# ScalarE copies of the FFN half tiles in batch 0, and accumulator banks lent to batch 1's first transposes

## The chip, the cores and the metric

One Trainium2 chip, of which the kernel uses a single core. The metric is the device time of one execution in microseconds (us); below two or three runs of the same kernel their median is given. A core has five engines that run side by side, each in its own program order: TensorE (PE, matrix products, its weight loads shown as PEld), VectorE (DVE), ScalarE (ACT), GpSimd (POOL) and SyncE (SP, which here issues nearly all DMAs).

## The reference

Inputs: `q`, `k`, `v` of shape (8 batches, 8 heads, 576 positions, 64), `p` of shape (8, 8, 32, 64), and two weight matrices `w_in` (512 x 2048) and `w_out` (2048 x 512) that arrive as 64-bit floats. All results are 32-bit.

```python
p_packed = sm_attn(p, k, v)              # 32 packed rows attend to 576 keys
out = sm_attn(q, p_packed, p_packed)     # 576 queries attend to the 32 packed rows
x = out.transpose(0, 2, 1, 3).reshape(B * S, H * D)        # 4608 x 512
h = x @ w_in
g = maximum(h, 0) + log1p(exp(-abs(h)))  # softplus
return g @ w_out
```

## The kernel before, in words

**The work.** The eight batches are taken one after the other. For a batch, `attention(b)` makes the softmaxed attention weights of the second attention (`aT`, split into a high and a low part `at_h`, `at_l` by `weights`), and `make_m` folds the packed rows into `w_in` (tiles `mh`, `ml`), so that the FFN's first product `h` is `m` times `at`. The FFN then runs over 16 tiles `f` of 128 hidden columns. Every large product is made of three products of rounded parts (high x high, high x low, low x high).

**A unit.** The main loop goes over units `u`, each a pair (batch, f); unit 0 is batch 0's tile 0 and unit 16 is batch 1's tile 0. In each unit these things are issued, in this order:

1. `gemm1` (line 581): 12 matmuls into two PSUM banks `ph`, one for each half of 288 positions. The pool `ps_h` has exactly two banks, so the next unit's `gemm1` writes the same two.
2. `softplus`, a chain of steps. Line 603: ScalarE takes `Abs` of each half out of PSUM into `e`. Lines 605 and 606: `Exp` and `Ln` on `e`, for batch 0 over both halves at once. Line 608: VectorE takes `max(h, 0) + e`, and reads `h` for it out of `ph` once more, so that both banks are held until line 608 has run. Later steps copy 64 columns aside on GpSimd (line 612) and split `e` into `gh` and `gl` on VectorE (lines 595, 596).
3. `gemm2_tile` (line 619) for the unit two before (`LAG = 2`): four accumulator tiles `acc`, 12 matmuls of 512 columns. The four banks of `ps_acc` hold them for a whole batch.
4. Between these four tiles, steps of the next batch's attention (`ahead`), and in batch 0 steps of `convert`.
5. After the unit, `make_m` for the unit two ahead, whenever a new slice of `m` begins: in batch 0 every second unit, 256 columns at a time (`psm`, line 544; read by ScalarE at line 559 and by VectorE at line 560).

**The PSUM banks.** Eight in all: four for `acc`, two for `ph`, and two (`ps_m`, tag "m") that everything else shares through `bank(...)`: the attention's transposes and scores, and `psm`. Before the first unit the list `spare` lends the accumulator banks to batch 0's attention; it is emptied (`spare.clear()`) ahead of unit 0.

**Batch 1's attention** runs inside batch 0's units. It begins with `transposed("k", 1, 0, hh)` for four `hh`: three transposes on TensorE (line 263) into one bank, and a ScalarE copy out of it (line 269, tile `T_k`). Two of them fall in unit 0, two in unit 1; the first scores that use them (line 276) come in unit 2, where the tiles `acc` of batch 0 are allocated too.

**The conversion.** `convert` turns the 64-bit weights into the 32-bit ones, 32 pieces in a fixed order (two of `w_in`, then two of `w_out`, and so on). A piece is a DMA into a buffer, two ScalarE activations (200, 204), two VectorE operations (206, 211), one GpSimd add (219), and for `w_out` another ScalarE (238) and VectorE (244) operation. It begins before unit 0 and ends in batch 0's last units.

**The order.** TensorE's instructions run in the order in which the program writes them. On the other engines a scheduler orders the instructions when the kernel is built, by priority (the order of the program) and by when it expects operands to be ready; on the chip each engine then runs its list in order. SyncE issues the loads in that way too.

Of the kernel before, what the change touches and what calls it, by code (L numbers as in the profile page):

```python
# [9 lines left out]
F32 = mybir.dt.float32  # L10
F32R = mybir.dt.float32r
AF = mybir.ActivationFunctionType
ALU = mybir.AluOpType
AX = mybir.AxisListType
I32 = mybir.dt.int32
# [11 lines left out]
def pack_attention_then_softplus_ffn(  # L27
# [10 lines left out]
    nc = tc.nc  # L38
    B, H, S, D = q.shape
    J = p.shape[2]  # L40
    DM, DFF = w_in.shape
    P = 128
# [3 lines left out]
    C = S // 2  # L46
# [9 lines left out]
    scale = 1.0 / math.sqrt(D)  # L56
# [4 lines left out]
    work = ctx.enter_context(tc.tile_pool(name="work", bufs=2))  # L61
    small = ctx.enter_context(tc.tile_pool(name="small", bufs=2))
    ps_acc = ctx.enter_context(tc.tile_pool(name="ps_acc", bufs=NT, space=bass.MemoryType.PSUM))
# [13 lines left out]
    def rest_at(b, f):  # L77

        return f + NF if f < LAG and b // 2 % 2 else f
# [3 lines left out]
    pT = const.tile([P, H, PW], F32, name="pT")  # L83

    spare = []

    def bank(nm):
        if spare:
            spare.append(spare.pop(0))
            pool, tag = spare[-1]  # L90
            return pool.tile([P, 512], F32, tag=tag, name=nm)
        return ps_m.tile([P, 512], F32, tag="m", name=nm)
# [24 lines left out]
    def load(nm, b, g):  # L117
        if b >= B:
            return
        src = {"q": q, "k": k, "v": v}[nm][b, g * HG:(g + 1) * HG]  # L120
        if b < FIRST:
            if (nm, b) == ("q", 0):
                o = DFF - (g + 1) * SI * D
                t = w_in_sb[:NP, :, o:o + SI * D].rearrange("x h (s d) -> x h s d", d=D)
            else:
                t = ld.tile([NP, HG, SI, D], F32, tag="ld", name=f"{nm}_{b}_{g}")
            nc.sync.dma_start(
                t.rearrange("x h s d -> x h (s d)"),
                src.rearrange("h (x s) d -> x h (s d)", s=SI),
            )  # L130
        elif nm == "v":
            t = ld.tile([NP, HG, SI, D], F32, tag="ld", name=f"{nm}_{b}_{g}")
            nc.sync.dma_start(
                t.rearrange("x h (m c) d -> x (h m) (c d)", c=2),
                src.rearrange("h (m x c) d -> x (h m) (c d)", x=NP, c=2),
            )
        else:
            t = ld.tile([P, HG, C], F32, tag="ld", name=f"{nm}_{b}_{g}")
            by_quad = src.rearrange("h (n x c) (e d) -> c e x (h n) d", x=Q, c=2, d=Q)
            for i in range(P // Q):  # L140
                nc.sync.dma_start(
                    t[i * Q:(i + 1) * Q].rearrange("x h (n d) -> x (h n) d", d=Q),
                    by_quad[i // 2, i % 2],
                )
        loaded[nm, b, g] = t
# [112 lines left out]
    def transposed(nm, b, g, hh):  # L258

        src = loaded[nm, b, g]  # L260
        ps = bank(f"psT_{nm}_{b}_{g}_{hh}")
        for i in range(HS):
            nc.tensor.transpose(
                ps[:, i * NP:(i + 1) * NP],
                src[:, hh, 2 * i:2 * i + 2, :].rearrange("x s d -> x (s d)"),
                ident[:NP, :NP],
            )
        dst = work.tile([P, C], F32, tag="T", name=f"T_{nm}_{b}_{g}_{hh}", bufs=4)
        nc.scalar.copy(dst, ps[:, :C])  # L269
        return dst  # L270
# [245 lines left out]
    def attention(b):  # L516
        return attention_first(b) if b < FIRST else attention_next(b)
# [18 lines left out]
    def make_m(b, c, res):  # L536


        n = m_cols(b)
        pss = [bank(f"psm_{b}_{c}_{g}") for g in range(G)]  # L540
        for g, ps in enumerate(pss):
            for hh in range(HG):
                o = D * g
                nc.tensor.matmul(  # L544
                    ps[hh * J:(hh + 1) * J, :n],
                    res["pt"][g][o:o + D, hh * J:(hh + 1) * J],
                    w_in_sb[o:o + D, hh, c * n:(c + 1) * n],
                    start=True, stop=True,
                )
        pool, th, tl = (cv, "t", "r") if b and c % 2 == 0 else (work, "mh", "ml")  # L550
        halves = []
        for g, ps in enumerate(pss):
            o = g * n % MC
            if o == 0:
                mh = pool.tile([P, MC], F32R, tag=th, name=f"mh_{b}_{c}_{g}", bufs=2)
                ml = pool.tile([P, MC], F32R, tag=tl, name=f"ml_{b}_{c}_{g}", bufs=2)
                halves.append((mh, ml))
            cols = slice(o, o + n)
            nc.scalar.copy(mh[:, cols], ps[:, :n])  # L559
            nc.vector.tensor_tensor(  # L560
                ml[:, cols], ps[:, :n], mh[:, cols].bitcast(F32), op=ALU.subtract
            )
        res["m"][c] = halves
# [24 lines left out]
    def halves(nm):  # L588
        return [
            work.tile([P, NT * P], F32R, tag=t, name=f"{t}_{nm}", bufs=LAG + 1)  # L590
            for t in ("gh", "gl")
        ]

    def split(hi, lo, x):
        nc.vector.tensor_copy(hi, x)  # L595
        nc.vector.tensor_tensor(lo, x, hi.bitcast(F32), op=ALU.subtract)  # L596

    def softplus(b, f, hv, done):
        e = work.tile([P, S], F32, tag="e", name=f"e_{b}_{f}")
        es = [e[:, c * C:(c + 1) * C] for c in range(2)]  # L600
        spans = [e] if b == 0 else es
        for c in range(2):
            nc.scalar.activation(es[c], hv[c], AF.Abs)  # L603
            for x in spans[c:c + 1] if b else spans[:c]:
                nc.scalar.activation(x, x, AF.Exp, scale=-1.0)  # L605
                nc.scalar.activation(x, x, AF.Ln, bias=1.0)  # L606
        for c in range(2):
            nc.vector.scalar_tensor_tensor(es[c], hv[c], 0.0, es[c], op0=ALU.max, op1=ALU.add)  # L608
        yield
        yield  # L610
        r = (b % 2) * REST
        nc.gpsimd.tensor_copy(rest[:, rest_at(b, f), r:r + REST], e[:, NT * P:])  # L612
        yield
        done[b, f] = halves(f"{b}_{f}")
        split(*done[b, f], e[:, :NT * P])
# [58 lines left out]
        order.append(("o", f))  # L674
    PACE = 0.56
    FRONT = 1000
    PACE_FIRST = 0.62
    CONV = 1.6
    CONV_EARLY = 1.6
# [18 lines left out]
    for st in range(NF * NT):  # L698
        with tc.high_priority(offset=FRONT):
            if next(steps, steps) is steps:  # L700
# [5 lines left out]
    for nm in ("k", "v"):  # L706
        for g in range(G):
            load(nm, 1, g)
    with tc.high_priority(offset=FRONT):
        make_m(0, 0, res[0])  # L710
# [4 lines left out]
    gs, acc = {}, None  # L715
    units = [(b, f) for b in range(B) for f in range(NF)]
    ahead, chain, due = iter(()), iter(()), 0.0
    for u in range(len(units) + LAG):
        if u < len(units):
            b, f = units[u]  # L720
            if f == 0:
                if (b + 1) % BG == 0 and b + 1 < B:
                    pack_transposed((b + 1) // BG, pt)
                ahead = attention(b + 1) if b + 1 < B else iter(())
                due = 0.0
            chain = softplus(b, f, gemm1(b, f, res[b]), gs)
            next(chain)
            if f == NF - 1:
                if (b + 2) % BG == 0 and b + 2 < B:
                    pt = load_pack((b + 2) // BG, (nc.sync,))  # L730
                for _ in ahead:
                    pass
                if b + 1 < B:
                    weights(b + 1)
        if u >= LAG:
            b2, f2 = units[u - LAG]
            gh, gl = gs.pop((b2, f2))
            if f2 == 0:
                acc = [ps_acc.tile([P, DM], F32, tag="acc", name=f"acc_{b2}_{t}") for t in range(NT)]
        last = u >= LAG and f2 == NF - 1 and b2 % 2 == 1  # L740
        if last:
            both = rests(b2)
            next(both)
        for t in range(NT):
            if u >= LAG:
                gemm2_tile(
                    acc[t], gh, gl, f2, slice(t * P, (t + 1) * P), f2 == 0, f2 == NF - 1
                )
                if f2 == NF - 1:
                    store(acc[t], [(0, b2, t * P, P)], f"{b2}_{t}", t)  # L750
            if u < len(units):
                due += PACE if b != FIRST - 1 else PACE_FIRST
                while due >= 1:
                    next(ahead, None)
                    due -= 1
                if b == 0:
                    cdue += CONV
                    while cdue >= 1:
                        next(conv, None)
                        cdue -= 1  # L760
            next(chain, None)
        if last:
            next(both)
        if u + 2 < len(units):


            nb, c = units[u + 2][0], units[u + 2][1] * P
            if c % m_cols(nb) == 0:
                make_m(nb, c // m_cols(nb), res[nb])
# [29 lines left out]
```

## Time and profile before

| | |
|---|---|
| time, median of 3 runs | 772.9 us (772.86 to 773.84) |
| the profiled execution | 772.78 us, its span 771.0 us |
| mean granted TensorE clock | 0.973 of full speed |
| TensorE busy | 733.0 us, 95% of the span |
| VectorE busy | 527.6 us, 68% |
| ScalarE busy | 434.8 us, 56% |
| GpSimd busy | 99.1 us, 13% |
| DMA | 55.97 MB moved, mean 73 GB/s |

The shares are means over the whole span. Batch 0 (its first `gemm1` starts at 39.16 us, batch 1's first at 151.55 us) looks different from the seven batches after it, so the table tells little of the stage that the change touches; that stage has to be read from views with a time window. Times of a view count from the span's start.

### The profile page before, as it was taken

The numbers are of one execution on the slowest core, as the hardware profiler recorded it, in microseconds if no ns is written. First come the engines' busy times: TensorE is split into PE (matmuls) and PEld (weight loads), VectorE is DVE, ScalarE is ACT, GpSimd is POOL, SyncE is SP. The second block draws the span as 40 slices with busy tenths as digits, with TensorE's granted clock in tenths as the row PEclk, the third lists the DMA queues.
The fourth block names the chain that finished last, engine by engine and source line by source line (L and its number), as shares of the span: only waits on it lengthen the run. The fifth ranks groups of instructions, "written<-read, shape, count | busy, mean of one in ns | idle before, by whom it ended". The sixth has DMA issues, their size and how long they took to land.

```text
span 771.0 us, 14168 instructions
## 1 busy us (share of the span) xinstructions
PE 733.0 (95%) x5360; PEld 579.5 (75%) x5360; DVE 527.6 (68%) x1092; ACT 434.8 (56%) x1057; POOL 99.1 (13%) x166
## 2 busy tenths in 40 slices
PE   6657998999999999999999999999999999999997
PEld 3445775887787778878788777878787777888886
DVE  2697879965877569565967559575867558565554
ACT  5668877766454545565555455565555355555540
POOL 1143444200000000000000000000010000000110
PEclk9559999999999999999999999999999999999999
DMA  9978655434403341052302342052402400010002
GB/s 211 237 185 190 185 137 150 95 76 73 93 1 76 56 81 44 1 124 47 79 1 76 55 64 61 1 109 42 91 2 61 70 1 1 1 55 1 1 1 68
DMA packets 149668, 55.97 MB, mean 73 GB/s; under 512 B 116320, under 2 KB 142944, under 8 KB 149600
## 3 DMA queue, kind: packets, MB, share of 16 engines
q1 hardware_dynamic: 149328, 55.00, 31.9%
q8 instruction: 42, 0.69, 0.4%
q14 instruction: 26, 0.21, 0.1%
q10 hardware_dynamic: 272, 0.07, 0.0%
HBM read 45.61 MB, written 9.44 MB: 71 GB/s over the span
## 4 chain that ended last, share of the span: by engine, by line
PE 85%; DVE 6%; ACT 4%; DMA 3%; issue 1%; POOL 1%; SPq 0%; ACTq 0%; DVEq 0%; POOLq 0%
PE acc L619 42%; PE ph L581 26%; PE acc_m L619 6%; PE psm L544 4%; PE ps L276 2%; DMA w_in_sb<-in_q 2%; PE psp L319 2%; PE psa L309 1%; DVE at_l L527 1%; DVE e L608 1%; DVE t L206 1%; ACT e L605 1%; DVE t L211 1%; ACT e L603 1%; DMA k<-in_k 1%
## 5 line engine op out<-in xcount | busy, mean ns | idle before, releaser
L603 ACT ACTIVATE e<-ph 128x288 f32<-128x288 f32 x256 | 103.2, 404 | 190.4 <-PE ph L581 143.4
L619 PE MATMUL acc<-wo_h,gh 128*128 128x512 f32 x512 | 208.0, 406 | 0.0
L608 DVE SCALAR_TENSOR_TENSOR e<-ph,e 128x288 f32<-128x288 f32 x256 | 113.4, 451 | 132.4 <-ACT e L606 131.3
L619 PE MATMUL acc<-wo_l,gh 128*128 128x512 f32 x512 | 201.2, 393 | 0.0
L619 PE MATMUL acc<-wo_h,gl 128*128 128x512 f32 x512 | 201.0, 393 | 0.0
L581 PE MATMUL ph<-at_h,mh 128*128 128x288 f32 x512 | 159.0, 311 | 12.7 <-ACT at_h L526 6.6
L581 PE MATMUL ph<-at_l,mh 128*128 128x288 f32 x512 | 153.6, 300 | 3.7 <-DVE at_l L527 3.7
L581 PE MATMUL ph<-at_h,ml 128*128 128x288 f32 x512 | 152.9, 299 | 0.0
L581 PEld LDWEIGHTS ph<-at_h,mh 128*128 128x128 f32 x512 | 97.9, 191 | 46.7 <-DVE gl L596 9.6
L612 POOL COPY rest<-e 128x64 f32<-128x64 f32 x128 | 53.8, 420 | 577.3 <-DVE e L608 547.7
L619 PEld LDWEIGHTS acc<-wo_h,gh 128*128 128x128 f32 x512 | 96.4, 188 | 27.5 <-issue 10.2
L619 PEld LDWEIGHTS acc<-wo_h,gl 128*128 128x128 f32 x512 | 96.3, 188 | 21.1
L605 ACT ACTIVATE e<-e 128x288 f32<-128x288 f32 (+1 forms) x240 | 109.4, 456 | 4.0
L606 ACT ACTIVATE e<-e 128x288 f32<-128x288 f32 (+1 forms) x240 | 109.4, 456 | 3.2
L619 PEld LDWEIGHTS acc<-wo_l,gh 128*128 128x128 f32 x512 | 96.6, 189 | 13.1
L581 PEld LDWEIGHTS ph<-at_l,mh 128*128 128x128 f32 x512 | 98.1, 192 | 8.1 <-DVE at_l L527 5.3
L581 PEld LDWEIGHTS ph<-at_h,ml 128*128 128x128 f32 x512 | 98.1, 192 | 0.0
L596 DVE TENSOR_TENSOR gl<-e,gh 128x512 fp32r<-128x512 f32 x128 | 87.7, 685 | 5.5
L559 ACT CAST mh<-psm 128x512 fp32r<-128x512 f32 (+1 forms) x72 | 35.9, 539 | 54.5 <-PE psm L544 54.3
L595 DVE CAST gh<-e 128x512 fp32r<-128x512 f32 x128 | 55.5, 434 | 5.5 <-DVE e L608 0.5
L560 DVE TENSOR_TENSOR ml<-psm,mh 128x512 fp32r<-128x512 f32 (+1 forms) x72 | 42.8, 623 | 20.6 <-ACT mh L559 20.0
L544 PE MATMUL psm<-w_in_sb,pt 64*32 64x512 f32 (+1 forms) x576 | 41.3, 567 | 7.6 <-ACT T_k L269 4.8
(79 smaller groups left out, 696.4 us busy)
## 6 DMA issues: line engine op xcount, KB each, us to landing
v<-in_v SPq DMA_DIRECT2D x16, 576.0 KB, 4.9
x_i<-in_moe_w_in SPq DMA_DIRECT2D x28, 256.0 KB, 4.4
k<-in_k SPq DMA_DIRECT2D x48, 144.0 KB, 3.2
q<-in_q SPq DMA_DIRECT2D x48, 144.0 KB, 3.1
x_o<-in_moe_w_out SPq DMA_DIRECT2D x11, 512.0 KB, 3.8
out<-o SPq DMA_DIRECT2D x18, 256.0 KB, 2.5
rest<-in_moe_w_out SPq DMA_DIRECT2D x5, 512.0 KB, 6.1
k<-in_k SPq DMA_DIRECT2D x4, 576.0 KB, 6.7
```

Of the source, the lines that this page charges most:

```text
L544: nc.tensor.matmul(ps[hh * J:(hh + 1) * J, :n], res["pt"][g][o:o + D, hh * J:(hh + 1) * J], w_in_sb[o:o + D, hh, c * n:(c + 1) * n], start ...
L559: nc.scalar.copy(mh[:, cols], ps[:, :n])
L560: nc.vector.tensor_tensor(ml[:, cols], ps[:, :n], mh[:, cols].bitcast(F32), op=ALU.subtract)
L581: nc.tensor.matmul(ph[:, :C], x[:, ms], y[:, g, cs], start=(i == 0), stop=(i == 3 * G - 1),)
L595: nc.vector.tensor_copy(hi, x)
L596: nc.vector.tensor_tensor(lo, x, hi.bitcast(F32), op=ALU.subtract)
L603: nc.scalar.activation(es[c], hv[c], AF.Abs)
L605: nc.scalar.activation(x, x, AF.Exp, scale=-1.0)
L606: nc.scalar.activation(x, x, AF.Ln, bias=1.0)
L608: nc.vector.scalar_tensor_tensor(es[c], hv[c], 0.0, es[c], op0=ALU.max, op1=ALU.add)
L612: nc.gpsimd.tensor_copy(rest[:, rest_at(b, f), r:r + REST], e[:, NT * P:])
L619: nc.tensor.matmul(acc, x[:, cs], y[:, f, :], start=(first and i == 0), stop=(last and i == 2),)
```

## The change

Two edits.

- **`softplus` in batch 0** (`OUT = 16`, so all its tiles). ScalarE copies both halves of `ph` into an SBUF tile `x` of 576 columns. VectorE takes the absolute value of all of `x` in one instruction, by masking the sign bit, into `e`. ScalarE's `Exp` and `Ln` follow as before. VectorE's last step is one instruction of 576 columns over `x` and `e`, in place of two of 288 that read `ph`. The tiles `x` use buffers of the attention that lie idle then: those of `aT` for f below 9, those of `a1` from 9 on. Batches 1 to 7 are as they were.
- **`transposed` in batch 1**, as long as `fresh` is not empty, that is until unit 2 allocates `acc`: its transposes go to the four banks of `ps_acc` in place of the two shared ones. Four such tiles fall in that time, one for each bank.

```diff
+    fresh = [None]
...
     def transposed(nm, b, g, hh):
         src = loaded[nm, b, g]
-        ps = bank(f"psT_{nm}_{b}_{g}_{hh}")
+        if b and fresh:
+            ps = ps_acc.tile([P, 512], F32, tag="acc", name=f"psT_{nm}_{b}_{g}_{hh}")
+        else:
+            ps = bank(f"psT_{nm}_{b}_{g}_{hh}")
...
-    def softplus(b, f, hv, done):
+    def softplus(b, f, phs, done):
+        hv = phs
         e = work.tile([P, S], F32, tag="e", name=f"e_{b}_{f}")
         es = [e[:, c * C:(c + 1) * C] for c in range(2)]
         spans = [e] if b == 0 else es
-        for c in range(2):
+        if b == 0 and f < OUT:
+            x = work.tile(
+                [P, S], F32, tag="aT" if f < 9 else "a1", name=f"x_{b}_{f}", bufs=2
+            )
+            hv = [x[:, c * C:(c + 1) * C] for c in range(2)]
+            for c in range(2):
+                nc.scalar.copy(hv[c], phs[c])
+            nc.vector.tensor_scalar(
+                e.bitcast(I32), x.bitcast(I32), 0x7FFFFFFF, None, op0=ALU.bitwise_and
+            )
+            nc.scalar.activation(e, e, AF.Exp, scale=-1.0)
+            nc.scalar.activation(e, e, AF.Ln, bias=1.0)
+            hv, es, spans = [x], [e], []
+        for c in range(2 if spans else 0):
             nc.scalar.activation(es[c], hv[c], AF.Abs)
             for x in spans[c:c + 1] if b else spans[:c]:
                 nc.scalar.activation(x, x, AF.Exp, scale=-1.0)
                 nc.scalar.activation(x, x, AF.Ln, bias=1.0)
-        for c in range(2):
-            nc.vector.scalar_tensor_tensor(es[c], hv[c], 0.0, es[c], op0=ALU.max, op1=ALU.add)
+        for x, y in zip(es, hv):
+            nc.vector.scalar_tensor_tensor(x, y, 0.0, x, op0=ALU.max, op1=ALU.add)
...
+    OUT = 16
...
             if f2 == 0:
+                fresh.clear()
                 acc = [ps_acc.tile([P, DM], F32, tag="acc", name=f"acc_{b2}_{t}") for t in range(NT)]
```

## The prediction

> **What bounds the kernel now.** I read the page's head first, then busy times by stage, then TensorE's waits in batch 0, then the rows of the engines around each wait.
>
> ```profile
> span 771.0 us, 14168 instructions
> PE 733.0 (95%) x5360; PEld 579.5 (75%) x5360; DVE 527.6 (68%) x1092; ACT 434.8 (56%) x1057; POOL 99.1 (13%) x166
> ```
>
> The sum below is made against this execution: span 771.0, time 772.78, so 1.8 us lie around the span; it is 0.1 below the median of 772.9. By stage (column two is the length, then the busy time of each engine and the granted clock):
>
> ```profile
> core 0: us, PE busy (x) PEld busy (x) DVE busy (x) ACT busy (x) POOL busy (x), PEclk, DMA share, GB/s
> 39.00:66.00 27.00, 16.00 (x86) 11.90 (x87) 22.41 (x34) 17.11 (x35) 12.47 (x10) 0.60 0.81 192
> 66.00:101.00 35.00, 32.71 (x268) 23.99 (x266) 29.18 (x62) 30.99 (x69) 15.98 (x15) 1.00 0.67 176
> 101.00:152.00 51.00, 47.53 (x369) 36.31 (x370) 45.81 (x95) 37.77 (x77) 18.44 (x19) 0.97 0.53 129
> 152.00:760.00 608.00, 606.76 (x4368) 486.07 (x4367) 409.40 (x853) 325.04 (x828) 46.08 (x113) 1.00 0.23 48
> ```
>
> From 152 us on TensorE is busy for 606.76 of 608 us: it is the bound there, and a microsecond by which batch 1's FFN starts earlier or later is a microsecond of the result. All that the change can do is done between 39 and 152 us. There TensorE is idle for 11.0, 2.3 and 3.5 us in the three stages, and the other engines are no longer idle company: VectorE is busy for 97.4 of 113 us, ScalarE for 85.9. TensorE's waits from 39 to 152 us, largest causes:
>
> ```profile
> PE ph L581 <- DVE e L608: 6.0, 4, 3.1
> PE psm L544 <- ACT T_k L269: 4.8, 2, 2.8
> PE psm L544 <- POOL w_in_sb L219: 1.7, 1, 1.7
> ```
>
> The first two rows, 10.8 us, are what the two edits are aimed at: `ph` held until line 608, and `psm` held up by a shared bank that a `T_k` copy has not emptied. Where they sit (start, length, engine, line; in brackets the idle time in front):
>
> ```profile
> 46.33 1.16 PE L263 MATMUL psT_k<-ident,k 96*128 96x96 f32 x6
> 50.28 1.08 PE L544 MATMUL psm<-w_in_sb,pt 64*32 64x256 f32 x8 [2.79 <-ACT T_k L269]
> 53.35 1.08 PE L544 MATMUL psm<-w_in_sb,pt 64*32 64x256 f32 x8 [1.98 <-ACT T_k L269]
> 54.36 0.61 PE L581 MATMUL ph<-at_h,mh 128*128 128x288 f32 x1
> ...
> 57.23 0.66 PE L263 MATMUL psT_k<-ident,k 96*128 96x96 f32 x6
> 60.95 0.61 PE L581 MATMUL ph<-at_h,mh 128*128 128x288 f32 x1 [3.05 <-DVE e L608]
> ...
> 63.93 0.39 PE L619 MATMUL acc<-wo_h,gh 128*128 128x512 f32 x1
> ...
> 75.53 0.40 PE L581 MATMUL ph<-at_h,mh 128*128 128x288 f32 x1 [1.81 <-DVE e L608]
> ...
> 77.23 0.40 PE L619 MATMUL acc<-wo_h,gh 128*128 128x512 f32 x1
> ...
> 134.27 0.67 PE L544 MATMUL psm<-w_in_sb,pt 64*32 64x256 f32 x16 [1.65 <-POOL w_in_sb L219]
> ```
>
> The two waits for `e` not shown make up the rest of the 6.0: 6.0 - 3.05 - 1.81 = 1.1 us.
>
> **Part 1, the lent banks.** What the four first `T_k` copies and the halves' reads looked like on ScalarE, and what VectorE and GpSimd did around them:
>
> ```profile
> 46.57 0.41 ACT L603 ACTIVATE e<-ph 128x288 f32<-128x288 f32 x1 [1.03 <-PE ph L581]
> ...
> 49.76 0.38 ACT L269 COPY T_k<-psT_k 128x288 f32<-128x288 f32 x1
> ...
> 57.43 0.41 ACT L603 ACTIVATE e<-ph 128x288 f32<-128x288 f32 x1
> ...
> 60.24 0.41 ACT L269 COPY T_k<-psT_k 128x288 f32<-128x288 f32 x1
> ```
>
> ```profile
> 55.88 1.13 DVE L206 TENSOR_SCALAR t<-m 128x512 int32<-128x512 int32 x1
> 56.93 0.41 DVE L560 TENSOR_TENSOR ml<-psm,mh 128x256 fp32r<-128x256 f32 x1
> ...
> 60.44 0.82 DVE L608 SCALAR_TENSOR_TENSOR e<-ph,e 128x288 f32<-128x288 f32 x2
> ```
>
> With the transposes in `ps_acc`, `psm` follows them on TensorE at once. Both waits go, 2.79 + 1.98 = 4.77 us, so unit 1's `gemm1` moves from 54.36 to about 49.6. What is late next there is already in place: the second half's bank is read by 46.98 (46.57 + 0.41). Moved with the edit are 12 transposes and four ScalarE copies in their old places; no DMA and nothing of SP's or POOL's queue moves. The new dependence is the accumulators' first matmul on the last of these copies: 60.65 against 63.93 now, and the copies move forward with the transposes. I cost it at nothing; without that cover it is at most the wait removed, 2.8 us.
>
> **Part 2, `ph` released by a copy.** Unit 2's `gemm1` waits 3.05 us for line 608. After the change the copies release `ph`: the row at 57.43, 0.41 long, ends at 57.84, and 4.8 us earlier after part 1, at 53.0. TensorE itself would be there at 57.89 - 4.8 = 53.1. But unit 2 is the first to use the second slice of `m`, and its last `ml` is finished by VectorE at 57.34. VectorE is busy for 22.41 of these 27 us; if its order stays and one added operation (0.36 us, below) lies ahead, `ml` comes at 57.7. So unit 2 starts between 53.1 (`ml` drawn forward with `psm`) and 57.7. I take 57.7, the row that exists: the lead at unit 2 is 60.95 - 57.7 = **3.2 us**, with 7.8 as the other end. Part 1's 4.8 us do not add to it; they turn into a wait for `ml`.
>
> The waits of 1.81 us (unit 4) and 1.1 us go in the same way, 2.9 us, if the copies run in time.
>
> **Part 3, what the added work costs.** Groups by shape from 39 to 152 us (busy us, mean ns):
>
> ```profile
> L211 DVE SCALAR_TENSOR_TENSOR t<-m,t 128x512 int32<-128x512 int32 x28 | 19.0, 682 | 0.3
> L206 DVE TENSOR_SCALAR t<-m 128x512 int32<-128x512 int32 x27 | 15.8, 587 | 6.0 <-ACT m L200 4.3 <-POOL r L219 1.4
> L244 DVE TENSOR_TENSOR wo_l<-r,wo_h 128x512 fp32r<-128x512 f32 x15 | 13.5, 905 | 1.8 <-POOL r L219 1.7
> L608 DVE SCALAR_TENSOR_TENSOR e<-ph,e 128x288 f32<-128x288 f32 x32 | 13.2, 447 | 6.2 <-ACT e L606 6.2
> ```
>
> ```profile
> L603 ACT ACTIVATE e<-ph 128x288 f32<-128x288 f32 x32 | 13.0, 412 | 11.3 <-PE ph L581 11.0
> ...
> L269 ACT COPY T_k<-psT_k 128x288 f32<-128x288 f32 x8 | 3.1, 392 | 0.7 <-PE psT_k L263 0.7
> ```
>
> ScalarE: 32 `Abs` of 412 ns become 32 copies; the copy of the same shape takes 392. That saves 0.6 us in all, which I drop. The new point is that `Exp` now waits for VectorE's absolute value. Behind it in ScalarE's order stand `Ln`, conversions, `T` copies and `mh`, for which TensorE waits. Bounds: nothing if conversion work fills the gap, and one mask at the longest of line 206's rows below, 1.52 us a unit. ScalarE has 27 us idle in the 113 and 16 x 1.52 = 24 would still fit into that, so I take nothing; without that cover all 24 us would lie on the path.
>
> VectorE, without waits: one mask of 576 columns, from line 206. Its rows split into quiet and long ones; the quiet median is below, 428 ns, so 428 x 576/512 = 0.48 us. One line-608-like operation of 576 from SBUF, by line 211's 682 x 1.125 = 0.77, replaces 2 x 0.447 = 0.89. Net 0.48 - 0.13 = **0.36 us a unit**.
>
> ```profile
> L206 DVE TENSOR_SCALAR t<-m x28: 399/428/1520, 38.4 to 140.1; 128x512 int32<-128x512 int32 x28
> L608 DVE SCALAR_TENSOR_TENSOR e<-ph,e x30: 410/448/459, 51.6 to 146.2; 128x288 f32<-128x288 f32 x30
> 55.13 1.59 POOL L219 TENSOR_TENSOR w_in_sb<-t,r 128x512 int32<-128x512 int32 x1 [1.36 <-DVE t L211]
> ```
>
> With waits: line 206 (SBUF to SBUF) has a minimum of 399 and a maximum of 1520 ns, line 608 (with PSUM) stays between 410 and 459. The long one at 55.88 started inside the GpSimd add that runs from 55.13 to 56.72, and ended 0.29 us after it. So operations between SBUF tiles wait out a GpSimd add, and the one with a PSUM operand does not. The change turns 32 of the immune kind into 32 of the other. Price of one: from 0 to 0.22 (line 244, 905 against a median of 684 in its own rows); line 206 pays 587 - 428 = 0.16. For two of them a unit the bounds are 0 and 0.44; I take 0.18, near line 206's, since the second kind (line 211) shows none. That makes 0.54 a unit.
>
> The Trainium skill, "SBUF — State Buffer", section "Who interferes with whom", speaks against this change: a VectorE instruction with two SBUF inputs, or in a two-port mode, and a GpSimd instruction that reads SBUF exclude each other for the whole instruction. By that rule the new last step is exposed as well as the mask, and the sum would use the upper bound of 0.44; the trace agrees for line 206, and for line 211 no long row shows it.
>
> **The sum.** Units 3 to 15 lie between 66 and 152 us. VectorE is busy there for 29.18 + 45.81 = 75.0 of 86 us. Thirteen units add 13 x 0.54 = 7.0, so 82.0. How full can VectorE get? The densest stretch I find is
>
> ```profile
> 120.00:140.00 20.00, 17.28 (x120) 13.31 (x119) 18.73 (x39) 15.18 (x32) 7.33 (x7) 0.91 0.46 109
> ```
>
> that is 94%, where TensorE already waits. At 95% the stage needs 82.0 / 0.95 = 86.3 us, 0.3 more than now. So the 2.9 us of waits taken away inside it come back as waits for VectorE's results (`psm` for the conversion as at 134.27, `gl`, `T`), and the lead of unit 2 is what is left: -3.2 + 0.3 = -2.9 us, **769.9 us** against 772.78. At no port waits the stage needs (75.0 + 4.7) / 0.95 = 83.9, a gain of 5.3 (767.5); at 0.80 a unit, (75.0 + 10.4) / 0.95 = 89.9, a loss of 0.7 (773.5). A measurement of this kernel can tell about 0.2%, 1.5 us.
>
> **The rivals.** (a) *All waits go.* VectorE's order follows the earlier `psm`, `ml` is ready and unit 2 starts at 53.1; with 7.8 there and 2.9 later, less up to 2 us of VectorE, 9 us: 764. For it: the scheduler orders VectorE anew. Against: the load just worked out. The clock goes the same way: it is 0.60 in the first stage, and unit 2's `gemm1` takes 63.93 - 60.95 = 2.98 us there, where unit 4's takes 77.23 - 75.53 = 1.70. The Trainium skill, "TensorE: Matmul & The Clock Gate", Part 1, says that one sustained busy window of about 3.4 us frees the clock; by it, a TensorE that idles less from 46 us on would run unit 2 warm, 2.98 - 1.70 = 1.3 us more. The rows agree on the slow clock; no run yet shows its release there.
>
> (b) *No change.* The lead is lost as well: VectorE and ScalarE (30.99 of 35 us busy from 66 to 101) cannot run 3 us ahead, and the conversion of the last `w_in` piece is late by as much more. 772.5.
>
> (c) *Slower.* VectorE becomes the bound through the port: every mask and every last step meets a GpSimd add. It decides from (75 + 13c) / 0.95 = 86 + 3.2 + 1.5 on, c = 0.86 us a unit; at 1.0 it is 92.6, a loss of 3.4: 776.2. For it: line 244's mean. Against: GpSimd is busy for 46.9 of 113 us, so less than half of the operations should meet it.
>
> **How the numbers follow.** My forecast (1.5 to 6 us gained) 0.45, rival (a) 0.17, (b) 0.21, (c) 0.17. Faster is the first two, 0.62; same 0.21; slower 0.17. The range runs from 764 (a's centre) to 774.3 (between b and c), which leaves out some 0.2; my own case alone is 766.8 to 771.3.
>
> **What would show it.** Right: `psm` without a wait for `T_k`, no wait of `ph` for the last softplus step, `gemm1` of unit 2 waiting for `ml` at about 57.7, VectorE above 92% from 66 to 152, batch 1's first `gemm1` 2.9 us earlier than now. Wrong: `ml` ready by 53 and unit 2 there (too little gain), last steps or masks of over 1 us as a rule, or ScalarE's `Exp` standing idle for VectorE with TensorE waiting behind it (too much).

## The result, and the profile after

The changed kernel takes **780.71 us** (median, 780.5 to 781.6) against 772.9 us (771.49 to 773.84): ratio 1.0107, 95% interval 1.0096 to 1.0119. It is **7.8 us slower**; the forecast was 769.9 us, with a range up to 774.3.

In the kernel after, line 581 of before is 585 (`gemm1`), 544 is 548 (`psm`), 560 is 564, 263 is 267, 269 is 273, 219 is 220, 206 is 207, 211 is 212, 244 is 245, 608 is 626. New are the copies out of PSUM (613) and the mask (614); batch 0's `Exp` and `Ln` are 617 and 618. The profiled execution took 780.71 us. The page's head, and the busy times by stage (columns as in the prediction):

```profile
span 778.9 us, 14157 instructions
PE 735.7 (94%) x5360; PEld 581.2 (75%) x5360; DVE 540.7 (69%) x1092; ACT 435.2 (56%) x1057; POOL 99.5 (13%) x166
```

```profile
39.00:66.00 27.00, 18.08 (x111) 12.42 (x110) 25.91 (x36) 17.66 (x37) 12.59 (x10) 0.71 0.79 189
66.00:101.00 35.00, 30.84 (x241) 23.31 (x238) 29.99 (x58) 28.68 (x63) 15.11 (x14) 0.95 0.60 159
101.00:152.00 51.00, 41.53 (x320) 32.04 (x319) 46.84 (x82) 34.02 (x69) 19.20 (x18) 0.90 0.47 117
152.00:760.00 608.00, 606.74 (x4388) 485.01 (x4387) 412.02 (x857) 330.60 (x838) 46.42 (x114) 1.00 0.23 48
```

The first stage did what the change says: TensorE is busy for 18.08 us in place of 16.00. TensorE's busy time is 1.9 us less in the second and 6.0 us less in the third, and from 152 us on nothing differs. So the loss lies between 66 and 152 us. The start of each unit's `gemm1` in the two timelines shows how it builds up (us from the span's start; unit 16 is batch 1's first):

```
unit      0      1      2      3      4      5      6       9      11      12      13      16
before  39.16  54.36  60.95  68.51  75.53  83.10  88.87  108.31  120.94  126.85  134.87  151.55
after   38.63  47.78  55.29  66.01  71.05  80.76  89.29  109.34  122.80  128.64  142.27  159.19
gain     0.5    6.6    5.7    2.5    4.5    2.3   -0.4    -1.0    -1.9    -1.8    -7.4    -7.6
```

A lead of 5.7 us at unit 2 is real. It is gone by unit 6, and between units 12 and 13 another 5.6 us are lost at one place. From the start of unit 0 to that of unit 16, first after and then before (columns as above):

```profile
38.63:159.19 120.56, 98.02 (x719) 73.07 (x719) 109.44 (x187) 85.47 (x177) 47.15 (x43) 0.88 0.60 148
39.16:151.55 112.39, 95.78 (x719) 71.75 (x719) 96.79 (x188) 85.77 (x177) 46.88 (x43) 0.89 0.64 159
```

The stretch is 8.2 us longer. TensorE is idle for 22.5 us of it in place of 16.6, and its 719 matmuls take 2.2 us longer, at a lower granted clock. Where the lead goes, from unit 2 to unit 6 (34.00 us against 27.92), the slower matmuls are the larger part: 30.34 us busy at a clock of 0.86 against 26.11 at 0.95.

TensorE's waits of after, from 39 to 152 us (us in total, times, longest; of the rows left out the waits for `at_h` and `at_l` in unit 0, 6.6 and 2.5 us, are the same in both kernels):

```profile
PE psm L548 <- POOL w_in_sb L220: 6.9, 1, 6.9
...
PE ph L585 <- ACT x L613: 5.1, 1, 5.1
...
PE psm L548 <- ACT a1T L314: 1.5, 2, 0.7
PE ps L280 <- ACT T_q L273: 1.4, 1, 1.4
PE psp L323 <- ACT a1T L314: 1.1, 1, 1.1
```

`psm`'s 4.8 us for `T_k` and `ph`'s 6.0 us for `e` are gone. In their place stand a wait for the new copies `x`, small waits for ScalarE's copies out of the shared banks, and above all the wait for the last piece of `w_in`: 1.7 us before, 6.9 now. What stands at that place on VectorE and GpSimd (start, length, engine, line):

```profile
125.71 1.29 POOL L220 TENSOR_TENSOR r<-t,r 128x512 int32<-128x512 int32 x1 [2.25 <-DVE t L212]
...
126.14 1.18 DVE L614 TENSOR_SCALAR e<-x 128x576 int32<-128x576 int32 x1
...
129.00 1.29 POOL L220 TENSOR_TENSOR r<-t,r 128x512 int32<-128x512 int32 x1 [2.00 <-DVE z L366]
129.16 1.75 DVE L626 SCALAR_TENSOR_TENSOR e<-x,e 128x576 f32<-128x576 f32 x1
...
135.63 1.27 POOL L220 TENSOR_TENSOR w_in_sb<-t,r 128x512 int32<-128x512 int32 x1 [3.96 <-DVE t L212]
135.81 1.71 DVE L626 SCALAR_TENSOR_TENSOR e<-x,e 128x576 f32<-128x576 f32 x1
...
138.10 0.41 DVE L207 TENSOR_SCALAR t<-m 128x512 int32<-128x512 int32 x1
...
139.59 1.58 POOL L220 TENSOR_TENSOR w_in_sb<-t,r 128x512 int32<-128x512 int32 x1 [1.78 <-DVE t L212]
...
141.23 0.68 PE L548 MATMUL psm<-w_in_sb,pt 64*32 64x256 f32 x8 [6.92 <-POOL w_in_sb L220]
```

The mask at 126.14 takes 1.18 us where its median is 0.45; it starts inside GpSimd's addition from 125.71 to 127.00 and ends 0.32 us after it. The last step at 129.16 starts inside GpSimd's addition from 129.00 to 130.29 and ends at 130.91, 0.62 us after it; the one at 135.81 ends 0.62 us after the addition that ends at 136.90. Both stand ahead of the piece's own work at 138.10, which TensorE waits for until 141.17. In this stretch VectorE has hardly any time left (same columns as the stages):

```profile
120.00:140.00 20.00, 13.71 (x100) 9.93 (x98) 19.93 (x37) 14.58 (x29) 7.07 (x8) 0.91 0.53 130
```

That is 19.93 of 20 us, where the kernel before had 18.73 (its own fullest 20 us, 116.5 to 136.5, had 19.55). Over the stage from 66 to 152 us VectorE is busy for 76.8 of 86 us, 89%. The mask and the new last step over the whole of batch 0 (minimum, median and maximum in ns; the groups' means are 672 and 999 ns):

```profile
L614 DVE TENSOR_SCALAR e<-x x16: 441/452/1540, 47.1 to 157.7; 128x576 int32<-128x576 int32 x16
L626 DVE SCALAR_TENSOR_TENSOR e<-x,e x16: 696/758/1747, 51.8 to 159.6; 128x576 f32<-128x576 f32 x16
```

In the timeline these 32 operations fall into two kinds. Ten of them, four masks and six last steps, start while an addition runs; all ten take 1.15 us or more, and end 0.32 us (mask) or 0.61 to 0.62 us (last step) after the addition. The other 22 take 0.76 us or less, also the eight of them during which an addition starts.

### The profile page after: what moved, and what is told of

The parts are those of the page before. It is cut to its first block, busy times and chain, and to the rows that moved or that the text cites. A ratio compares the mean times of both kernels' runs of the same rounds, so it can differ in the third digit from the quotient of the medians.

```text
span 778.9 us, 14157 instructions
## 1 busy us (share of the span) xinstructions
PE 735.7 (94%) x5360; PEld 581.2 (75%) x5360; DVE 540.7 (69%) x1092; ACT 435.2 (56%) x1057; POOL 99.5 (13%) x166
## 4 chain that ended last, share of the span: by engine, by line
PE 82%; DVE 9%; ACT 4%; DMA 2%; issue 1%; POOL 1%; SPq 0%; ACTq 0%; POOLq 0%; DVEq 0%
PE acc L637 41%; PE ph L585 25%; PE acc_m L637 6%; PE psm L548 4%; PE ps L280 2%; DMA w_in_sb<-in_q 2%; PE psp L323 1%; DVE t L212 1%; PE psa L313 1%; DVE at_l L531 1%; DVE e L626 1%; DVE wo_l L245 1%; DVE t L207 1%; DVE gh L599 1%; PE psT_q L267 1%
## 5 line engine op out<-in xcount | busy, mean ns | idle before, releaser
L621 ACT ACTIVATE e<-ph 128x288 f32<-128x288 f32 x224 | 90.2, 403 | 178.5 <-PE ph L585 131.6
L626 DVE SCALAR_TENSOR_TENSOR e<-ph,e 128x288 f32<-128x288 f32 x224 | 100.0, 451 | 126.6 <-ACT e L624 125.5
L623 ACT ACTIVATE e<-e 128x288 f32<-128x288 f32 x224 | 98.4, 439 | 3.6
L624 ACT ACTIVATE e<-e 128x288 f32<-128x288 f32 x224 | 98.4, 439 | 3.1
L600 DVE TENSOR_TENSOR gl<-e,gh 128x512 fp32r<-128x512 f32 x128 | 89.5, 699 | 5.5
```

Source lines behind the costliest of these rows:

```text
L626: nc.vector.scalar_tensor_tensor(x, y, 0.0, x, op0=ALU.max, op1=ALU.add)
```

## The experiments

Unit numbers are by the start of `gemm1`. The kernels of one group shared a chip and the runs of the kernel before (772.2 to 772.8 us). In the expectations, theory H is the hand-off of the mask between ScalarE and VectorE, L the mask's load on VectorE, T and O the place of the `w_in` pieces in the order, P the port that VectorE shares with GpSimd, and D the additions' own time in the chain of a piece.

### Each part alone

The two parts were separated, the copies were cut to three tiles, and the mask was given back to ScalarE:

```diff
-    OUT = 16            # e1_banks_only:  OUT = 0
-        if b and fresh: # e2_copies_only: if False
-    OUT = 16            # e3_first_three: OUT = 3
-            nc.vector.tensor_scalar(e.bitcast(I32), x.bitcast(I32), 0x7FFFFFFF, None, op0=ALU.bitwise_and)
+            nc.scalar.activation(e, x, AF.Abs)   # e4_abs_on_scalar
```

> Only the lent banks, softplus as before. Theory P (port: the mask and the last step over SBUF tiles wait out GpSimd adds, 0.46 us a unit, and push the weight conversion back) and theory H (hand-off: ScalarE's Exp waits for VectorE's mask and the conversion's activations stand behind it) both put the whole loss on the copies, so both expect no loss here: between 770 and 773 us, psm without its 4.8 us of waits for T_k, the wait of psm for the last w_in piece at 1 to 3 us. If the lent banks themselves do harm (order on the engines changed for the worse), it is over 775.

> Only the copies, transposes in the shared banks. P and H: the loss of the changed kernel, 6 to 11 us over before (779 to 784), with masks and last steps of mean 0.65 and 1.0 us and a wait of 5 us or more for the last w_in piece. If the loss needs both edits, it is below 776.

> Both edits, the copies only in the first 3 of 16 tiles. The changed kernel was 4.5 us ahead at unit 4 and lost 12 us after it. P and H: 13 of 16 sources of loss are gone, the lead is kept: 768 to 771 us, unit 4 at 71 to 72 us, the wait for the last w_in piece 1 to 4 us. If the early lead alone drags the conversion into lateness, it comes back to 772 or more.

> As changed, but the absolute value of the copied tile is taken by ScalarE (0.68 us an instruction, 11 us more on it) and not by VectorE. H: no wait of Exp for VectorE is left, most of the loss goes: 772 to 776. P: VectorE loses 0.67 us a unit of masks with their port waits, but the last step still waits 0.24 on average; about half of the loss goes: 775 to 778. If neither and ScalarE becomes the bound: over 781.

| kernel | us | ratio to before, 95% interval |
|---|---|---|
| banks only | 773.97 | 1.0021 (1.0011 to 1.003) |
| copies only | 782.05 | 1.0126 (1.0111 to 1.0141) |
| both, three tiles | 772.19 | 0.999 (0.9978 to 1.0002) |
| both, abs on ScalarE | 775.57 | 1.0037 (1.0024 to 1.005) |

The lent banks do not cost the loss and bring nothing alone; the 774.0 lies 1 us above what was expected of them. TensorE's waits in that kernel, 35 to 165 us:

```profile
PE ph L585 <- DVE e L626: 9.9, 7, 3.9
```

The 4.8 us for `T_k` turned into a longer wait for line 608's successor, 9.9 us in place of 6.0. The copies carry the whole loss. Three tiles keep the early lead to unit 4 (72.05 against 75.53) and have 0.7 us of it at unit 16 (150.84 against 151.55), so the 768 to 771 us expected of them were not reached. Giving the mask back to ScalarE takes back some 5 of the 7.8 us: the wait for the last piece falls to 0.2 us there, though the last step is still long at 1.0 us.

### Is it the mask: the hand-off from ScalarE to VectorE and back, or its load?

ScalarE's waits of after, 35 to 165 us, show the hand-off that the prediction took as nothing:

```profile
ACT e L617 <- DVE e L614: 10.4, 10, 2.6
```

So the mask was cut to 64 columns, with `Exp` still waiting for it, and then left out. In both, `Exp` reads `x` with a small scale, so the softplus of batch 0 is not computed.

```diff
-            nc.vector.tensor_scalar(e.bitcast(I32), x.bitcast(I32), ...)
-            nc.scalar.activation(e, e, AF.Exp, scale=-1.0)
+            nc.vector.tensor_scalar(e[:, :64].bitcast(I32), x[:, :64].bitcast(I32), ...)  # e8_small_mask only
+            nc.scalar.activation(e, x, AF.Exp, scale=-0.01)                               # both
```

> Both edits, but the mask covers 64 of 576 columns and Exp reads the copied tile itself at a small negative scale, so the softplus is not computed. Exp still has to wait for VectorE's small instruction (it writes into the same tile); VectorE's mask work falls from 0.45 to about 0.1 us. Theory H (Exp stands behind VectorE's queue): nearly all of the loss stays, 777 to 781. Theory L (what counts is VectorE's time, masks of 0.67 us with their port waits): most of the loss of the masks goes, 773 to 776, as with the absolute value on ScalarE.

> As the one before, without any mask: Exp reads the copied tile at once; the absolute value is left out. No hand-off to VectorE and no mask work; only the last step over SBUF tiles (1.0 us against 0.89 us before) is left of VectorE's extra. H and L both: 768 to 773. If the port wait of the last step alone carries the loss: 776 or more.

Measured: 777.96 us (1.0064, 1.0049 to 1.0079) with the small mask, 780.07 us (1.0094, 1.0077 to 1.0111) with none. Neither the hand-off nor the mask's load can be the cause by itself: with both gone, the loss stays. Two lines say more, VectorE's group in the kernel with the small mask (busy us, mean ns) and TensorE's wait in the one without:

```profile
L614 DVE TENSOR_SCALAR e<-x 128x64 int32<-128x64 int32 x16 | 9.8, 610 | 0.0
```

```profile
PE psm L548 <- POOL w_in_sb L220: 9.8, 3, 6.6
```

A ninth of the columns still takes 610 ns in the mean, against 672 for all 576. The shortest row of the small mask is 148 ns, so most of what this one pays is waiting; of the full mask's 672 ns it is 220. And without any mask `w_in` is late all the same. There the last step is all that is left on VectorE of the change, with a mean of 868 ns and a median of 752: its waits come to 16 x 0.116 = 1.9 us, in a kernel that loses 7.6. So the waits of the moved operations can't be added up into the loss either.

### Is it the order in which the pieces are converted?

The wait for the last `w_in` piece suggests converting these pieces sooner. In one pair of kernels they were put one pair of tiles earlier in the list, in the other pair every conversion step in batch 0's units got a higher priority; each edit was made to the kernel before as well.

```diff
+    order += [("i", 0), ("i", 1)]              # e5_order_after, e6_order_before
     for f in range(NF):
-        if f % 2 == 0:
-            order += [("i", f), ("i", f + 1)]
+        if f % 2 == 0 and f + 2 < NF:
+            order += [("i", f + 2), ("i", f + 3)]
...
-                        next(conv, None)
+                        with tc.high_priority(offset=50):   # e10_pieces_first_after, e11_pieces_first_before
+                            next(conv, None)
```

> The changed kernel with the weights' pieces in another order: each pair of w_in pieces is converted one pair of w_out pieces earlier. Theory T (the lost 8 us is the wait for the last w_in piece, because the conversion runs late while the w_out pieces ahead of it have time to spare): that 6.9 us wait goes and the time falls to 772 to 776. If VectorE's load over the whole stage is the bound, the wait comes back elsewhere (accumulators or ph) and the time stays at 778 to 782.

> The kernel before with the same order of pieces. T: its 1.7 us wait for the last w_in piece and the slow clock behind it (about 1.5 us) go: 769 to 771. VectorE-bound: no change, 772 to 774.

> The changed kernel, with the conversion's steps in batch 0 given a higher priority in the scheduler (by 50 instructions), so that on ScalarE and VectorE the last two w_in pieces stand about one unit of softplus earlier; no instruction is added or left out. Theory O (the order on ScalarE's and VectorE's lists decides, not the added work: the kernel without masks had the same 6.6 us wait and the same late place of the last w_in piece): the 6.9 us wait goes to under 1.5 us, the time falls to 772 to 777. If VectorE's work bounds the stage whatever the order: the wait moves to ph, acc or the shared banks and the time stays at 779 or more.

> The kernel before with the same priority for the conversion. O: its 1.7 us wait for the last w_in piece goes, with the slow clock behind it: 769 to 772. If earlier conversion steps stand in the way of line 608, which frees ph: 774 or more.

| edit | changed kernel | kernel before |
|---|---|---|
| earlier in the list | 785.5 us, 1.0163 (1.0141 to 1.0184) | 775.99 us, 1.0041 (1.003 to 1.0053) |
| higher priority | 784.85 us, 1.0162 (1.0145 to 1.0178) | 775.91 us, 1.0052 (1.0035 to 1.0069) |

The earlier list brings a cost of its own: TensorE waits for the load of `k`, 4.8 us in the changed kernel and 4.9 in the kernel before. All four kernels are slower than without the edit, and with the earlier list both lie above either expectation. The wait for `w_in` is gone in both changed kernels, and the distance between the two of a pair stays: 9.5 and 8.9 us. The time moved to other waits. With the higher priority, in the changed kernel from 39 to 152 us:

```profile
PE psp L323 <- ACT a1T L314: 3.9, 1, 3.9
...
PE psm L548 <- ACT T_q L273: 2.3, 1, 2.3
PE psm L548 <- DVE pt L338: 1.5, 1, 1.5
PE psm L548 <- DVE a L348: 1.5, 1, 1.5
```

So the late piece is where the loss shows, not what makes it. These runs also give a measure of disorder: a different order alone moved the kernel before by 3.5 and 3.7 us, and the changed one by 4.8 and 4.1.

### Is it GpSimd's additions and the port?

GpSimd's additions were cut to 64 of 512 columns, in both kernels. The numbers of `w_in` are zero or unfinished then; a fill at the start gives the tile defined contents.

```diff
+    nc.gpsimd.memset(w_in_sb[...], 0.0)        # two fills at the start
...
+            k = CN // a // 8
             nc.gpsimd.tensor_tensor(
-                dst ..., *v, op=ALU.add
+                dst[:, :, :k], *[y[:, :, :k] for y in v], op=ALU.add
             )
```

> The kernel before with GpSimd's conversion adds cut to an eighth of their columns (the other weights stay unconverted or zero; two memsets at the start fill w_in). Each add goes from 1.3 to about 0.2 us, so VectorE's waits for the port all but vanish. Port theory P: VectorE's long rows (about 10 us in all) go and the time falls by 2 to 4 us, to 769 to 771. If the port waits are hidden: 772 to 774.

> The changed kernel with the same cut. P: mask and last step come down to 0.45 and 0.76 us and the difference to the kernel before with the same cut falls from 8 us to under 2 us. O and L without port: the difference stays at 5 us or more.

Measured: before 767.17 us (0.994, 0.992 to 0.9961), changed **765.59 us** (0.9928, 0.9904 to 0.9953). The kernel before falls below the 769 to 771 us that were expected. The loss of 7.8 us is gone; the two differ by 1.6 us, less than these intervals tell apart. TensorE still waits for `w_in` in the changed kernel, three times and 6.4 us in all:

```profile
PE psm L553 <- POOL w_in_sb L225: 6.4, 3, 2.8
```

The two operations of the changed kernel now (minimum, median, maximum):

```profile
L631 DVE SCALAR_TENSOR_TENSOR e<-x,e x16: 745/758/874, 46.6 to 144.4; 128x576 f32<-128x576 f32 x16
...
L619 DVE TENSOR_SCALAR e<-x x16: 442/452/570, 43.4 to 142.1; 128x576 int32<-128x576 int32 x16
```

The medians are those of after to the nanosecond, and the maxima fell from 1747 to 874 and from 1540 to 570. In these two kernels long ones exist only while GpSimd has long additions. The Trainium skill, "SBUF — State Buffer", section "Who interferes with whom", names both kinds, a VectorE instruction with two SBUF inputs and a `tensor_scalar` in a two-port mode, and says that the one that comes second is blocked for the whole instruction; the rows at 126.14, 129.16 and 135.81, the ten of 32 above and these maxima agree with it for both.

A short addition shortens the conversion of a piece too. So a second pair kept the additions at full length and took them out of the chain: their result goes to a buffer that TensorE does not read, `w_in` stays zero, and the residual of `w_out` is formed from the number ahead of the addition.

```diff
-            if w == "i":
-                dst, a = w_in_sb.bitcast(I32)[:, :, i * P:(i + 1) * P], DM // P
...
-                    wo_l[:, i, :], rs[n - 1].bitcast(F32), wo_h[:, i, :].bitcast(F32),
+                    wo_l[:, i, :], t, wo_h[:, i, :].bitcast(F32),
```

> The kernel before, with GpSimd's 512-column additions at their full length, but with their results put aside: the pieces of w_in stay zero from a fill at the start, and the residual of w_out is formed from the number as it stood ahead of the addition. So VectorE still shares its port with the same additions, and TensorE waits for none of them. Theory P (the port): 766 to 775 us, as before, with the residual near 0.84 us in the mean. Theory D (the additions' own 1.3 us in the chain from piece to TensorE): 767 to 769 us, as with the short additions.

> The same in the changed kernel. Theory P: it stays 5 to 9 us above the run before it here, near 778, with the last step near 1.0 us in the mean and ScalarE's Exp waiting 10 us for the mask in all; psm's 6.9 us wait for the last piece of w_in is gone and its time turns up in other waits. Theory D: the difference falls to between -2 and +1 us, as with the short additions, although the last step stays near 1.0 us.

Measured: before 774.96 us (1.0025, 1.0014 to 1.0036), changed 778.94 us (1.0069, 1.0048 to 1.009): 4.0 us apart, between the two expectations. VectorE's last step in the changed one:

```profile
L626 DVE SCALAR_TENSOR_TENSOR e<-x,e x16: 737/758/1821, 49.8 to 158.4; 128x576 f32<-128x576 f32 x16
```

The long ones are back, and with them a loss, though TensorE waits for no addition's result. Step by step, after minus before is -1.6 us with short additions, +4.0 with long ones beside the chain, +7.8 with long ones in it. That the 7.8 became 4.0 is no work of the changed kernel: from unit 0's start to unit 16's it takes 121.09 us, about as without the edit (120.56). It is the kernel before that takes 117.66 us there in place of 112.39, and it starts unit 0 3.2 us earlier (the changed one 2.3). With short additions the same stretch takes 109.94 us before and 108.14 changed.

So the loss goes with the long additions: the 9.4 us between the ends are well above the 3.5 to 4.8 us that an order of its own is worth. How much of it is their hold on VectorE, and how much the lists that the scheduler makes around them, these pairs do not tell; each of these edits also changed the order on VectorE and ScalarE.

### How many tiles?

If the price is paid tile by tile, a few tiles should keep the lead.

```diff
-    OUT = 16
+    OUT = 2        # c2_two; 4 in c3_four, 8 in c4_eight; 3 in c1, with nc.scalar.activation(e, x, AF.Abs) for the mask
```

> The changed kernel with the copies for three tiles alone and |x| of these made by ScalarE. If the three masks on VectorE (3 x 0.67 us, before the port fills) cost what the three tiles lose: 770.5 to 771.5 us. If three tiles of lead are given back at the conversions whatever makes the mask: 772 to 773 us, as with three tiles and the mask on VectorE. A third way, ScalarE's three added Abs (3 x 0.6 us) delay the copies of T_k and T_q: 773 to 774.5 us.

> The changed kernel with the copies for two tiles alone, those whose banks the second half's transposes used to wait for. If each tile past the second only loads VectorE: 771 to 772 us, a little under the kernel before. If the lead is given back at the conversions: 772.2 to 773.2 us.

> The changed kernel with the copies for four tiles alone. With none it was 774.0, with two 777.6, with three 772.2, with sixteen 780.7 us. If each copied tile costs its share of VectorE's added time (8.5 us over the 13 tiles past the third, 0.65 us a tile): 772.9 us. If what decides is where the waits fall in the lists that each count gives, not the count: anything from 771 to 778 us, and off that line by over 1.5 us.

> The same with eight tiles. By the share of VectorE's added time: 772.2 + 5 x 0.65 = 775.5 us. By the lists: off that by over 1.5 us, either way.

| tiles copied | 0 | 2 | 3 | 3, abs on ScalarE | 4 | 8 | 16 |
|---|---|---|---|---|---|---|---|
| us | 773.97 | 777.57 | 772.19 | 772.62 | 776.68 | 779.07 | 780.71 |
| ratio to before | 1.0021 | 1.0055 | 0.999 | 0.9993 | 1.0058 | 1.0078 | 1.0107 |
| 95% interval | 1.0011 to 1.003 | 1.0039 to 1.0071 | 0.9978 to 1.0002 | 0.9977 to 1.0008 | 1.0039 to 1.0077 | 1.0061 to 1.0095 | 1.0096 to 1.0119 |

The time grows with the count, but not tile by tile: two and four tiles are 5.4 and 4.5 us above three, two lies outside both expectations, and four is 3.8 us off the line that the share of VectorE's added time gives, eight 3.6 us. Each count gets lists of its own from the scheduler, and I take it that where the waits fall in them is worth as much as the operations. No version in this table beats the kernel before.

## Why the prediction was wrong, step by step

- **Part 1 held.** `psm` does not wait for `T_k` at those places, and unit 1 starts at 47.78, against the 49.6 forecast (0.5 of it was there at unit 0). Its `gemm1` even runs at the fast clock, 49.48 - 47.78 = 1.70 us in place of 57.23 - 54.36 = 2.87.
- **Part 2 held in size, not in kind.** Unit 2 starts at 55.29, between the two ends (53.1 and 57.7). It does not wait for `ml`, as I said, but 5.15 us for the copies `x`, which ScalarE reaches late, behind a `T_k` copy, a conversion that waits for GpSimd, and `mh`:

```profile
52.52 0.38 ACT L273 COPY T_k<-psT_k 128x288 f32<-128x288 f32 x1
53.73 0.68 ACT L205 ACTIVATE r<-rest 128x512 int32<-128x512 uint32 x1 [0.84 <-POOL w_in_sb L220]
54.31 0.62 ACT L563 CAST mh<-psm 128x256 fp32r<-128x256 f32 x2
54.83 0.71 ACT L613 COPY x<-ph 128x288 f32<-128x288 f32 x2
```

  The lead was 5.7 us, more than my 3.2. "If the copies run in time" was the right doubt. That wait also let the clock fall: unit 2's `gemm1` takes 58.52 - 55.29 = 3.2 us, and unit 13's, after 6.92 us of waiting, 145.31 - 142.27 = 3.0.
- **ScalarE's cost, taken as nothing, was wrong as a step.** `Exp` stood idle for the mask for 10.4 us in all, within the bound of 24, with `T` copies, `a` and `a1T` behind it. But the kernel without the mask shows that the loss is there without it.
- **The price on VectorE was mis-sized.** I took 0.36 us a unit and 0.18 of port waits, 0.54. By the rows it is 0.672 + 0.999 - 2 x 0.447 = 0.78 us, of which (0.672 - 0.452) + (0.999 - 0.758) = 0.46 are waits, just above my upper bound of 0.44. The choice that failed is "near line 206's, since the second kind (line 211) shows none": the last step pays 0.24 us in the mean. Nor is line 211's kind safe: in the kernel before with the additions put aside one of its rows (213 there) takes 1649 ns, where the median is 679. The reading that I left to one sentence on the Trainium skill's page was the right one.
- **The sum failed as a method, and this is the step that turned the sign.** Put 0.78 into my own formula and the stage needs (75.0 + 10.1) / 0.95 = 89.6 us, 3.6 more; with the 3.2 of lead that is 773.2, still no loss to speak of, 7.5 us below the measured time. The step that failed is that VectorE's added work costs nothing until its mean fill over 86 us reaches 95%. VectorE is at 89% over the stage, and still 13.3 us are lost from unit 2, 5.7 ahead, to unit 16, 7.6 behind. Of these 8.6 us are added idle time of TensorE (14.38 against 5.76), and 4.7 us are slower matmuls (89.52 us busy against 84.84, at a clock of 0.91 against 0.97), for which the sum has no term. From 120 to 140 us VectorE is at 99.7%, where it was at 94% before: the last pieces of `w_in`, the attention of the next batch and the new operations meet there, and 5.6 of the 13.3 us are lost between units 12 and 13. The 94% was not the densest stretch either: from 77 to 85 us VectorE is busy for all of 8.00 us before.
- **The rivals.** (c) came nearest, "VectorE becomes the bound through the port", at 776.2 and a chance of 0.17, but its condition did not come about. It wanted every mask and every last step to meet an addition and 0.86 us a unit; ten of 32 were held up, as its reason against had it (less than half), the price was 0.78, and the loss came all the same. In the rows above, VectorE's own results release the additions (in brackets), so an addition starts just as VectorE goes on to its next operation, in the stretch where VectorE has no time left. (a) expected a faster clock; it came at unit 1 and not at unit 2, and no lead was kept.

What stays open is the way from the long additions to TensorE's idle time. The kernel with `Abs` on ScalarE is 4.5 us faster than the one that leaves the mask out, although it does more work; the one without the mask pays 1.9 us of waits in its last steps and loses 7.6; and three tiles are faster than two. I read all three as the order of the lists, which moves the kernel before by some 3.5 us as well, but this is not shown: no run fixes the lists and changes the operations alone.

## What to carry to other kernels

Moving an operand from PSUM to SBUF changes which engines the operation competes with, so price it from rows where a GpSimd operation overlaps, not from medians. Judge an almost full engine by its fullest 20 us ahead of the bound engine, not by the mean over a stage. And when an experiment removes the wait that looks guilty and the time stays, the wait was the place and not the cause: take away what feeds it.

## What the hardware showed that I had not expected

- What an operation over SBUF tiles pays does not go with its own size: 610 ns in the mean for a mask of 64 columns, 672 for 576, and 1.71 to 1.75 us for a last step that takes 0.76 alone.
- Cutting GpSimd's additions to an eighth is worth 5.0 us (772.21 to 767.17) to the kernel before, on an engine that the page shows busy for 13% of the span. In the profiled executions 3.3 us of the gain lie ahead of unit 0, which starts at 35.82 in place of 39.16.
- Whether a mask or a last step waited went with who started first: the ten that started during an addition took 1.15 us or more, the eight during which an addition started 0.76 us or less.
